# Four experts' results turned to rows by VectorE blocks and transfers in place of TensorE

## The chip, the core and the metric

The kernel runs on one core of a Trainium2 chip. The metric is the device time of one execution in microseconds (us). Engines are named as in the profile: PE is TensorE (its weight loads are PEld), DVE is VectorE, ACT is ScalarE, POOL is GpSimd, SP is SyncE, which only issues transfers here. "L889" is line 889 of the kernel. A difference of 0.2% is about 1.4 us here.

## The reference

An attention over 32 heads whose mask comes from sign hashes, followed by a mixture of experts over 3072 tokens of width 512. The change lies in the second part:

```
expert_idx = np.argmax(x @ w_gate, axis=1)           # 8 experts
for e in range(E):                                   # tokens sorted by expert
    h = np.maximum(x_sorted[lo:hi] @ w1[e], 0.0)     # 512 -> 1024
    y_sorted[lo:hi] = h @ w2[e]                      # 1024 -> 512
y = y_sorted[inv_perm]
return gate_w[:, None] * y
```

## The kernel before, in words

The first 410 us or so are the attention; while it ends, each token's row is written to the DRAM buffer `sorted_rows`, which has a region for each expert. Then the experts follow one after another in the order of how many tokens they have. Each has a fixed room (`CAPS`), and the list `PH` gives the phases: n = 0 and 1 are the largest expert in two parts of 256 tokens, n = 2 to 8 are the others with rooms for 456, 432, 408, 396, 384, 372 and 354 tokens.

The program is written out in a fixed order; each engine runs its instructions in that order and waits on semaphores. One phase n has two halves.

- **First product, `mm1(n, f)` for f = 0 to 7 (L823).** Each f is 12 matmuls of PE: 4 blocks of the depth by 3 products, since every factor is kept as a rounded value and a rest ("high" and "low") and the product of the two lows is dropped. The token block `xh` is the moving side, all tokens of the phase at once. ACT then writes the high part of `hh` (L837), DVE the low part (L839), and only then the PSUM buffer (name `s`, three of them) is free.
- **Second product, `mm2(n, m)`.** There are two forms. By token (`by_token`, rooms up to 384: phases 0, 1, 6, 7, 8) `hh` is the stationary side and the result comes out with tokens on partitions (L880). Otherwise, in the four phases n = 2 to 5 (rooms 456, 432, 408, 396), the weight is the stationary side and the result comes out as columns: 128 features on partitions, the tokens along the row (L860, 24 matmuls for each m = 0 to 3). ACT copies each to the tile `yt` (L864).

Where the result is in columns it must be turned to rows. Before, PE does it: `yout(n, j)` transposes four 128x128 blocks of `yt` into a PSUM buffer (L889), DVE scales them by the token's gate into a tile `y` (L894, three buffers), POOL sends the 128 rows to their places in the output with an indirect transfer (L896). For the four phases n = 2 to 5 these calls are spread over the next phase: after `mm1(n + 1, f)` for f = 1, 3, 5, 7.

Between these pieces stands the work for the next expert. `halves` brings its weights: SP loads half a megabyte into `raw` (L705, four buffers, three loads ahead), ACT writes the rounded part (L718), POOL the rest (L719). One such part stands behind every f of the first half of a phase, two behind every m of the second. `rows(n + 1)` loads the next tokens' rows into `xb` at the start of phase n (L735, four transfers, and `xg`, L740), and `xt_blocks(n + 1, ks)` turns them in the second half: DVE transposes 32x32 blocks (L773), ACT rounds (L774), DVE subtracts (L776). `w1p` is a second copy of w1 whose rows are in the order that these 32x32 blocks leave.

The same way of turning stands in the attention: DVE transposes 32x32 blocks (L349) and 16 transfers on SP's queue bring the blocks to other partitions (L355, `pt<-w`).

Of the kernel before, what the change touches and what calls it, by code (L numbers as in the profile page):

```python
# [7 lines left out]
F32 = mybir.dt.float32  # L8
# [13 lines left out]
DM = H * D  # L22
N = B * S
E = 8
F = 1024
# [14 lines left out]
EARLY = 256  # L40
# [11 lines left out]


@with_exitstack
def lsh_attention_moe(ctx, tc, qk, qk2, v, proj, wg, w1, w1p, w2, out):
    nc = tc.nc
    const = ctx.enter_context(tc.tile_pool(name="const", bufs=1))
    moe = ctx.enter_context(tc.tile_pool(name="moe", bufs=1))
# [494 lines left out]
    EV = {}  # L553
# [133 lines left out]
    def raw_load(c, a):  # L687

        r, k = divmod(c, 4)
        if k < 2:  # L690
            src = (w1p if r else w1)[bass.ds(EV[r], 1)].rearrange("o (a p) f -> p (o a) f", p=128)[:, 2 * a:2 * a + 2,
                                                                                k * 512:(k + 1) * 512]
        else:
            o = (k - 2) * 4 + 2 * a
            src = w2[bass.ds(EV[r], 1)].rearrange("o (a p) d -> p (o a) d", p=128)[:, o:o + 2, :]
        n = 2 * c + a
        if n in (2, 3):
            if n == 2:
                RAW["x"] = moe.tile([128, 2, 2, 512], F32, name="xhe")
            t = RAW["x"][:, a]  # L700
        elif n < 10 or n % 2:
            t = moe.tile([128, 2, 512], F32, name="raw", bufs=2)
        else:
            t = P2["p"].tile([128, 2, 512], F32, name="raw2", bufs=2)
        nc.sync.dma_start(t, src)  # L705
        RAW[c, a] = t
# [134 lines left out]
    def by_token(n):  # L841
        return PH[n][2] <= 384

    def mm2(n, m, mid=None):

        r, o, c = PH[n]
        if by_token(n):
            yout(n, m, mid)
            return
        if m == 0:  # L850
            YT[n] = (wk.tile([128, 4, EARLY], F32, name="qk") if n == 0 else
                     P2["p"].tile([128, 4, CAPS[1]], F32, name="yt"))
        h = HH[n]
        ms = slice(m * 128, (m + 1) * 128)
        p = ps.tile([128, 512], F32, name="s", bufs=3)
        k = 0
        for f in range(8):
            w = CH[4 * r + 2 + f // 4]
            for a, b in ((0, 0), (0, 1), (1, 0)):
                nc.tensor.matmul(p[:, :c], w[:, a, f % 4, ms], h[b][:, f, :c], start=(k == 0), stop=(k == 23))  # L860
                k += 1
                if k == 12 and mid:
                    mid()
        nc.scalar.activation(YT[n][:, m, :c], p[:, :c], AF.Copy)  # L864

    def yout(n, j, mid=None):
        r, o, c = PH[n]
        if j >= len(tiles_of(c)):
            return
        i, pw = tiles_of(c)[j]  # L870
        if n + 1 == len(PH) and j + 1 == len(tiles_of(c)):
            youts(n, j, i, pw)
            return
        p = ps.tile([128, 512], F32, name="s", bufs=3)
        if by_token(n):
            k = 0
            for f in range(8):
                w = CH[4 * r + 2 + f // 4]
                for a, b in ((0, 0), (1, 0), (0, 1)):
                    nc.tensor.matmul(p[:pw], HH[n][b][:, f, i:i + pw], w[:, a, f % 4],  # L880
                                     start=(k == 0), stop=(k == 23))
                    k += 1
                    if k == (12 if n else 20) and mid:
                        mid()
        else:

            yw = max(pw, min(128, CAPS[1] - i))
            for m in range(4):
                nc.tensor.transpose(p[:yw, m * 128:(m + 1) * 128], YT[n][:, m, i:i + yw], ident)  # L889
        if n:  # L890
            y = P2["p"].tile([128, DM], F32, name="y", bufs=3)
        else:
            y = moe.tile([128, DM], F32, name="y0")
        nc.vector.tensor_scalar(y[:pw], p[:pw], GT[n][:pw, j:j + 1], None, op0=OP.mult)  # L894
        nc.gpsimd.memset(C["spacer"], 0.0)
        st = nc.gpsimd.indirect_dma_start(out=out, out_offset=bass.IndirectOffsetOnAxis(ap=IX[n][:pw, j:j + 1], axis=0),  # L896
                                          in_=y[:pw], in_offset=None, bounds_check=N - 1, oob_is_err=False)
        for q in outs:
            tc.declare_no_dep(st.ins, q.ins, reason="rows of other tokens")
        outs.append(st)  # L900
# [280 lines left out]
    for n in range(1, len(PH)):  # L1181
# [3 lines left out]
            rows(n + 1)  # L1185
        for f in range(8):
            mm1(n, f)
            if f % 2 and not by_token(n - 1):
                yout(n - 1, f // 2)
            halves(c0, f)  # L1190
            if 3 <= n < 6:
                for _ in range(2):
                    next(plan, None)
        for m in range(4):
            if not last:
                xt_blocks(n + 1, ((0, 1), (2,), (3,), ())[m] if not by_token(n) else ((0, 1), (2, 3), (), ())[m])
            if not (last and m == 3):
                mm2(n, m)
            halves(c0 + 2, 2 * m)
            halves(c0 + 2, 2 * m + 1)  # L1200
        if n == 6:
# [72 lines left out]
```

## Time and profile before

| | before |
|---|---|
| median of 3 runs | 700.62 us (700.34 to 700.83) |
| the profiled execution | 699.71 us, of which the span from first to last instruction 697.8 |
| PE busy | 688.8 us (99% of the span) |
| DVE, ACT, POOL busy | 444.6, 434.3, 466.8 us (64, 62, 67%) |
| chain that ended last | PE 92%, of it 1% L889 |

A busy share of an engine says how long it had an instruction running. The chain is followed back from the last instruction to what released each step. In the four phases n = 2 to 5 and what follows them the profile page shows PE at 99% in every slice, and the clock that was granted to it at full.

### The profile page before, as it was taken

What the parts mean: (1) busy time and instruction counts of PE and PEld (TensorE: products, weight loads), DVE (VectorE), ACT (ScalarE), POOL (GpSimd) and SP (SyncE); (2) the same over time, 40 slices, a digit from 0 to 9 for tenths busy, and PEclk for the clock granted to TensorE, in tenths of its full rate; (3) what the DMA queues carried; (4) which work ended last, traced back from release to release, by engine and by line L of the source; (5) the groups of instructions that cost most, each with busy time, mean ns of one, the idle gap of its engine ahead of it and who ended that gap; (6) DMA issues with size and microseconds to landing.
All of it is one profiled execution on the core that took longest, in us unless ns stands there. A gap on an engine that the chain in (4) does not pass through costs nothing.

```text
span 697.8 us, 12285 instructions
## 1 busy us (share of the span) xinstructions
PE 688.8 (99%) x4219; PEld 564.7 (81%) x4219; DVE 444.6 (64%) x916; ACT 434.3 (62%) x866; POOL 466.8 (67%) x517
## 2 busy tenths in 40 slices
PE   8999999999999999999999999999999999999997
PEld 4778677867786778677876789899999999989896
DVE  8878787878787878788875645342939333363421
ACT  7988888878888888887876315443443444444310
POOL 7967755595796768876866436856666676758522
PEclk9999999999999999999999999999999999999999
DMA  7609777976778558764983158656355493738101
GB/s 285 160 19 261 208 219 210 269 187 219 254 230 222 154 132 224 223 202 143 257 274 129 65 184 248 170 177 155 127 163 170 131 181 123 210 124 234 61 10 42
DMA packets 64528, 123.09 MB, mean 176 GB/s; under 512 B 15329, under 2 KB 29025, under 8 KB 64400
## 3 DMA queue, kind: packets, MB, share of 16 engines
q1 hardware_dynamic: 56736, 103.17, 52.2%
q0 software_dynamic: 7584, 19.10, 8.6%
q8 instruction: 34, 0.56, 0.3%
q14 instruction: 30, 0.25, 0.1%
q10 hardware_dynamic: 144, 0.02, 0.0%
HBM read 65.75 MB, written 26.33 MB: 132 GB/s over the span
## 4 chain that ended last, share of the span: by engine, by line
PE 92%; issue 4%; POOL 1%; ACT 1%; DVE 1%; POOLq 0%
PE s L823 19%; PE t L389 18%; PE s L860 11%; PE s L297 10%; PE t L327 10%; PE s L299 9%; PE s L880 8%; PE t L409 3%; PE t L254 2%; PE s L889 1%; POOL w L719 1%; PE t L103 1%; ACT e L313 0%; POOL out_dram L896 0%; ACT pt L379 0%
## 5 line engine op out<-in xcount | busy, mean ns | idle before, releaser
L307 DVE TENSOR_SCALAR_CACHE_REDUCE e<-s 128x768 f32<-128x768 f32 x192 | 178.9, 953 | 61.3 <-PE s L299 56.5
L313 ACT ACTIVATE e<-e,m 128x768 f32<-128x768 f32 x192 | 177.9, 929 | 16.3 <-DVE e L307 12.4
L719 POOL TENSOR_TENSOR w<-raw,w 128x512 fp32r<-128x512 f32 x112 | 144.6, 1314 | 36.7 <-ACT w L718 35.5
L389 PE MATMUL t<-pt,vt 128*64 128x384 f32 x768 | 130.9, 490 | 0.0
L823 PE MATMUL s<-xh,w 128*128 128x456 f32 (+6 forms) x672 | 126.8, 346 | 0.0
L823 PEld LDWEIGHTS s<-xh,w 128*128 128x128 f32 x672 | 119.2, 188 | 3.0
L839 DVE SCALAR_TENSOR_TENSOR hh<-s,hh 128x256 fp32r<-128x256 f32 (+7 forms) x64 | 35.5, 555 | 107.5 <-ACT hh L837 107.5
L389 PEld LDWEIGHTS t<-pt,vt 128*64 128x64 f32 x768 | 52.3, 137 | 63.7 <-issue 63.2
L327 PE MATMUL t<-ident,e 128*128 128x128 f32 x648 | 92.1, 274 | 1.4 <-DVE pt L377 0.5
L379 ACT ACTIVATE pt<-t 128x512 f32<-128x512 f32 (+1 forms) x147 | 82.1, 581 | 16.4 <-PE t L327 15.3
L837 ACT ACTIVATE hh<-s 128x256 fp32r<-128x256 f32 (+7 forms) x64 | 31.3, 490 | 90.7 <-PE s L823 90.7
L327 PEld LDWEIGHTS t<-ident,e 128*128 128x128 f32 x648 | 76.6, 140 | 8.7 <-ACT e L313 1.8
L349 DVE STREAM_TRANSPOSE w<-e 128x768 f32<-128x768 f32 x84 | 79.0, 964 | 0.8 <-DMA pt<-w 0.6
L896 POOL DMA_INDIRECT out_dram<-y,ix x28 | 27.9, 996 | 73.1 <-DVE y L894 43.9
L860 PE MATMUL s<-hh,w 128*128 128x456 f32 (+3 forms) x384 | 74.9, 355 | 0.0
L860 PEld LDWEIGHTS s<-hh,w 128*128 128x128 f32 x384 | 71.1, 188 | 2.6
L718 ACT ACTIVATE w<-raw 128x512 fp32r<-128x512 f32 x112 | 66.3, 622 | 1.0 <-DMA raw<-in_w1p_dram 1.0
L880 PE MATMUL s<-w,hh 128*128 128x512 f32 (+1 forms) x240 | 56.4, 394 | 0.0
L297 PE MATMUL s<-w 80*128 80x384 f32 x192 | 55.1, 368 | 0.0
L297 PE MATMUL s<-qk 80*128 80x384 f32 x192 | 54.8, 367 | 0.0
L880 PEld LDWEIGHTS s<-w,hh 128*128 128x128 f32 (+1 forms) x240 | 44.6, 187 | 10.5
L299 PE MATMUL s<-qk 128*128 128x384 f32 x192 | 49.8, 340 | 0.0
(220 smaller groups left out, 979.9 us busy)
## 6 DMA issues: line engine op xcount, KB each, us to landing
pt<-w SPq DMA_DIRECT2D x224, 144.0 KB, 3.8
raw<-in_w_dram SPq DMA_DIRECT2D x34, 512.0 KB, 3.4
raw<-in_w1p_dram SPq DMA_DIRECT2D x28, 512.0 KB, 3.4
xd<-in_qk_dram SPq DMA_DIRECT2D x14, 768.0 KB, 7.1
sorted_rows<-xr SPq DMA_DIRECT2D x6, 1156.0 KB, 8.1
vt<-in_v_dram SPq DMA_DIRECT2D x16, 384.0 KB, 3.8
masks<-bits POOLq DMA_DIRECT2D x14, 192.0 KB, 3.8
sorted_rows<-sorted_rows SPq DMA_DIRECT2D x2, 1156.0 KB, 7.1
```

The lines of the kernel that those rows point to most:

```text
L297: nc.tensor.matmul(p[:, a, :HALF], k[0:80, 2, c], k[0:80, 3, n], start=i >= 4, stop=i < 4)
L299: nc.tensor.matmul(p[:, a, :HALF], k[:, 0, c], k[:, 1, n], start=i < 4, stop=i >= 4)
L307: nc.vector.tensor_scalar(e, SC.pop(i)[:, :, :HALF], CEIL, None, op0=OP.min, op1=OP.min, accum_out=m)
L313: nc.scalar.activation(e, e, AF.Exp, bias=m, scale=-1.0, accum_out=SM[g, hf][:, t, s:s + 1])
L327: nc.tensor.transpose(o[:, j, w], e[w][:, kt // 3, (kt % 3) * 128:(kt % 3) * 128 + 128], ident)
L349: nc.vector.transpose(z[:, :, c, w].rearrange("p g (k i) -> p g k i", i=32), e)
L379: nc.scalar.activation(o, x, AF.Copy)
L389: nc.tensor.matmul(p[s * 64:(s + 1) * 64, :HALF], VT[g][:, kt, s, :], PT[u][:, :, :, s, kt].rearrange("p a t i -> p t a i"), start=(kt == ...
L719: nc.gpsimd.tensor_tensor(w[:, 1, a], r, w[:, 0, a], op=OP.subtract)
L823: nc.tensor.matmul(p[:, :c], w[:, a, d, fs], x[:, b, d, :c], start=(k == 0), stop=(k == 11))
L860: nc.tensor.matmul(p[:, :c], w[:, a, f % 4, ms], h[b][:, f, :c], start=(k == 0), stop=(k == 23))
L880: nc.tensor.matmul(p[:pw], HH[n][b][:, f, i:i + pw], w[:, a, f % 4], start=(k == 0), stop=(k == 23))
```

## The change

The four `mm2` phases in columns keep their matmuls, but the turning to rows leaves PE. After each `mm2(n, m)` and ACT's copy to `yt`, DVE transposes `yt` in 32x32 blocks into a new tile `yb`. After m = 3, `y_rows` issues 16 transfers on SP's queue that carry the blocks between groups of 32 partitions into a new tile (same name, `yt`), in which the tokens are on partitions. DVE scales from there, no longer from PSUM. All four `yout` calls stand behind `mm1(n + 1, 7)`. A copy of w2 whose columns are ordered for this (`w2p`) is loaded for these four experts. POOL clears the few columns of `yt` beyond the tokens. In `xt_blocks` the third and fourth block are both turned at m = 1.

```diff
@@ raw_load
-            src = w2[bass.ds(EV[r], 1)].rearrange(...)[:, o:o + 2, :]
+            src = (w2 if r == 0 or by_token(r + 1) else w2p)[bass.ds(EV[r], 1)].rearrange(...)[:, o:o + 2, :]
@@ mm2
+        nb = -(-c // 32)
         if m == 0:
-            YT[n] = (wk.tile([128, 4, EARLY], F32, name="qk") if n == 0 else
-                     P2["p"].tile([128, 4, CAPS[1]], F32, name="yt"))
+            YT[n] = P2["p"].tile([128, 4, CB * 32], F32, name="yt")
+            YB[n] = P2["p"].tile([128, 4 * 4, 128], F32, name="yb")
+            nc.gpsimd.memset(YT[n][:, :, c:nb * 32], 0.0)
...
         nc.scalar.activation(YT[n][:, m, :c], p[:, :c], AF.Copy)
+        nc.vector.transpose(YB[n][:, :nb, 32 * m:32 * m + 32], YT[n][:, m, :nb * 32].rearrange("p (b j) -> p b j", j=32))
+    def y_rows(n):
+        c = PH[n][2]
+        nb = -(-c // 32)
+        YR[n] = P2["p"].tile([128, 4, DM], F32, name="yt")
+        y = YB[n].rearrange("p (t q) w -> p q t w", q=4)
+        for r in range(4):
+            for a in range(4):
+                q = (a + r) % 4
+                t = len(range(q, nb, 4))
+                nc.sync.dma_start(YR[n][32 * q:32 * q + 32, :t, 128 * a:128 * a + 128], y[32 * a:32 * a + 32, q, :t])
@@ yout
-            for m in range(4):
-                nc.tensor.transpose(p[:yw, m * 128:(m + 1) * 128], YT[n][:, m, i:i + yw], ident)
+            p = YR[n][:, j]
@@ the loop over phases
             mm1(n, f)
-            if f % 2 and not by_token(n - 1):
-                yout(n - 1, f // 2)
+            if f == 7 and not by_token(n - 1):
+                for j in range(4):
+                    yout(n - 1, j)
             halves(c0, f)
...
-                xt_blocks(n + 1, ((0, 1), (2,), (3,), ())[m] if not by_token(n) else ((0, 1), (2, 3), (), ())[m])
+                xt_blocks(n + 1, ((0, 1), (2, 3), (), ())[m])
             if not (last and m == 3):
                 mm2(n, m)
+            if m == 3 and not by_token(n):
+                y_rows(n)
             halves(c0 + 2, 2 * m)
             halves(c0 + 2, 2 * m + 1)
```

On PE the change only takes away. The first half of phase 5 (396 tokens) before, where `yt` holds the result of phase 4:

```order
L823 MATMUL s<-xh,w_6055 128x396 x24
L889 MATMUL s<-ident,yt 128x128 x4
L823 MATMUL s<-xh,w_6055 128x396 x24
L889 MATMUL s<-ident,yt 128x128 x4
L823 MATMUL s<-xh,w_6158 128x396 x24
L889 MATMUL s<-ident,yt 128x128 x4
L823 MATMUL s<-xh,w_6158 128x396 x24
L889 MATMUL s<-ident,yt 72x128 x4
```

And the same place now:

```order
L862 MATMUL s<-hh_6064,w_6000 128x408
L823 MATMUL s<-xh,w_6081 128x396 x48
L823 MATMUL s<-xh,w_6162 128x396 x48
L862 MATMUL s<-hh_6432,w_6295 128x396
L862 MATMUL s<-hh_6433,w_6295 128x396
```

The four L889 rows are gone, as in phases 3, 4 and 6, and the 96 L823 matmuls follow each other (L862 is the line that was L860).

On SP, the end of phase 2 and the start of phase 3 before, with the semaphores that each transfer waits for (DMAHW0 to 7 are the eight lanes on which SP's transfers report that they landed):

```order
L705 DMA raw<-in_w1p_dram 128x2x512 [waits DMAHW6_49,DMAHW2_49,Pool_49]
L705 ISA
L705 DMA raw_5640<-in_w1p_dram 128x2x512 [waits DMAHW7_49,DMAHW3_49,Pool_49]
L735 ISA
L735 DMA xb<-sorted_rows 32x13x128 [waits DVE_49]
```

And the same place now, the first 9 of the 16 transfers; the weight load of L705 and the four of L735 stand behind the last of them:

```order
L705 DMA raw<-in_w1p_dram 128x2x512 [waits DMAHW6_49,DMAHW2_49,Pool_49]
L881 DMA yt<-yb 32x4x128 [waits DMAHW7_49,DVE_49]
L881 DMA yt<-yb 32x4x128 x2
L881 DMA yt<-yb 32x3x128
L881 DMA yt<-yb 32x4x128 [waits DMAHW3_49]
L881 DMA yt<-yb 32x4x128 [waits DMAHW4_49]
L881 DMA yt<-yb 32x3x128 [waits DMAHW5_49]
L881 DMA yt<-yb 32x4x128 [waits DMAHW6_49]
L881 DMA yt<-yb 32x4x128 [waits DMAHW7_49]
```

The first of the 16 waits for DVE; the ninth reports on lane 7 again, as the first did, and waits until that one has landed.

On DVE, the end of the first half of phase 5 and its second half before (`y<-s` is the scaling, DMASW are the lanes of POOL's indirect transfers, whose landing frees a `y` buffer):

```order
L894 TENSOR_SCALAR y<-s,gate 128x512 [waits DMASW7_49,PE_49]
L839 SCALAR_TENSOR_TENSOR hh_6404<-s,hh_6403 128x396 [waits Activation_49] x2
L894 TENSOR_SCALAR y<-s,gate 24x512 [waits DMASW0_49,DVE_49,PE_49]
L769 COPY gate<-xg 128x3 [waits DMAHW6_49]
L751 COPY ix<-xg 128x3
L773 STREAM_TRANSPOSE xt<-xb 128x384 [waits DMAHW4_49,DMAHW5_49,DMAHW3_49,DMAHW2_49]
L773 STREAM_TRANSPOSE xt<-xb 128x384
L776 TENSOR_TENSOR xh<-xt,xh 128x384 [waits Activation_49] x2
L773 STREAM_TRANSPOSE xt<-xb 128x384
L776 TENSOR_TENSOR xh<-xt,xh 128x384 [waits Activation_49]
L773 STREAM_TRANSPOSE xt<-xb 128x384
L776 TENSOR_TENSOR xh<-xt,xh 128x384 [waits Activation_49]
```

And the same place now, from the third of the four scalings on:

```order
L908 TENSOR_SCALAR y<-yt,gate 128x512 [waits DMASW7_49]
L908 TENSOR_SCALAR y<-yt,gate 24x512 [waits DMASW0_49,DVE_49]
L769 COPY gate<-xg 128x3 [waits DMAHW6_49]
L751 COPY ix<-xg 128x3
L773 STREAM_TRANSPOSE xt<-xb 128x384 [waits DMAHW4_49,DMAHW5_49,DMAHW3_49,DMAHW2_49]
L773 STREAM_TRANSPOSE xt<-xb 128x384
L776 TENSOR_TENSOR xh<-xt,xh 128x384 [waits PE_49,Activation_49]
L776 TENSOR_TENSOR xh<-xt,xh 128x384 [waits Activation_49]
L867 STREAM_TRANSPOSE yb<-yt 128x13x32 [waits Activation_49,Pool_49]
L773 STREAM_TRANSPOSE xt<-xb 128x384 x2
L776 TENSOR_TENSOR xh<-xt,xh 128x384 [waits Activation_49] x2
L867 STREAM_TRANSPOSE yb<-yt 128x13x32 [waits Activation_49] x3
```

The four scalings now stand in a row, the fourth waiting for the transfer that the first one feeds (DMASW0), and the next tokens' transposes L773 and subtractions L776 stand behind them and, the second pair, behind a `yb` transpose too.

## Rows read from the trace of the kernel before

**Rows 1.** The page: span, busy times, PE's granted clock, and `pt` issues (KB, landing).

```profile
span 697.8 us, 12285 instructions
PE 688.8 (99%) x4219; PEld 564.7 (81%) x4219; DVE 444.6 (64%) x916; ACT 434.3 (62%) x866; POOL 466.8 (67%) x517
...
PEclk9999999999999999999999999999999999999999
...
pt<-w SPq DMA_DIRECT2D x224, 144.0 KB, 3.8
```

**Rows 2.** Groups by shape, 440 to 697.8 us: busy us, mean ns, idle before.

```profile
L889 PE MATMUL s<-ident,yt 128*128 128x128 f32 x48 | 7.2, 272 | 0.0
L889 PE MATMUL s<-ident,yt 128*72 128x128 f32 x16 | 2.4, 272 | 0.0
```

**Rows 3.** The chain that ended last, 440 us on: start, us, what.

```profile
478.95 4.71 PE s L823 x24
...
499.54 18.89 PE s L860 x96
518.43 4.49 PE s L823 x24
...
538.12 17.92 PE s L860 x96
556.04 4.32 PE s L823 x24
560.36 0.44 PE s L889 x4
...
575.10 17.34 PE s L860 x96
592.44 4.20 PE s L823 x24
...
611.01 16.67 PE s L880 x72
```

**Rows 4.** Busy by stretch (PE, PEld, DVE, ACT, POOL): phase 4's second half.

```profile
538.10:556.00 17.90, 17.90 (x98) 17.88 (x97) 9.49 (x16) 7.11 (x15) 11.70 (x10) 1.00 0.38 122
```

**Rows 5.** Groups by shape, 440 to 697.8 us, of DVE and POOL.

```profile
L896 POOL DMA_INDIRECT out_dram<-y,ix x25 | 24.9, 996 | 59.9 <-DVE y L894 30.6 <-PE s L823 5.7 <-DVE xt L773 4.6
L894 DVE TENSOR_SCALAR y<-s,gate 128x512 f32<-128x512 f32 x19 | 14.1, 744 | 17.4 <-PE s L880 17.4
L773 DVE STREAM_TRANSPOSE xt<-xb 128x448 f32<-128x448 f32 x4 | 2.4, 625 | 0.0
```

**Rows 6.** ACT in order of time, end of phase 5 and in phase 6: start, us.

```profile
592.48 0.50 ACT L864 ACTIVATE yt<-s 128x396 f32<-128x396 f32 x1 [2.79 <-PE s L860]
...
603.88 0.49 ACT L837 ACTIVATE hh<-s 128x384 fp32r<-128x384 f32 x1 [1.53 <-PE s L823]
604.26 0.62 ACT L718 ACTIVATE w<-raw 128x512 fp32r<-128x512 f32 x1
```

**Rows 7.** SP's issues in order of time, start of phase 6: start, us to the last's end.

```profile
592.37 1.89 SPq L735 DMA_DIRECT2D xb<-sorted_rows  x4
```

**Rows 8.** SP's issues in the attention: one group of 16 transfers.

```profile
50.94 11.20 SPq L355 DMA_DIRECT2D pt<-w  x16
```

**Rows 9.** Transfers, 470 to 660 us: KB each, median us to landing.

```profile
raw<-in_w1p_dram SPq DMA_DIRECT2D x19, 512.0 KB, 3.4
...
xb<-sorted_rows SPq DMA_DIRECT2D x8, 208.0 KB, 5.0
```

**Rows 10.** The indirect transfers to the output, whole span.

```profile
DMA to landing us min/median/max: 1.9/2.8/8.8
```

**Rows 11.** DVE in order of time, phases 4 and 5: start, us.

```profile
536.52 2.88 DVE L667 TENSOR_SCALAR ttt<-ttt,rof 128x24 f32<-128x24 f32 x1
...
577.73 2.16 DVE L776 TENSOR_TENSOR xh<-xt,xh 128x384 fp32r<-128x384 f32 x2 [0.19 <-ACT xh L774]
```

**Rows 12.** POOL in order of time, beside the first row above.

```profile
536.80 2.55 POOL L719 TENSOR_TENSOR w<-raw,w 128x512 fp32r<-128x512 f32 x2
```

More of the change, by code (lines that the diff above doesn't have):

```diff
@@ L54, in lsh_attention_moe @@
 @with_exitstack
-def lsh_attention_moe(ctx, tc, qk, qk2, v, proj, wg, w1, w1p, w2, out):
+def lsh_attention_moe(ctx, tc, qk, qk2, v, proj, wg, w1, w1p, w2, w2p, out):
     nc = tc.nc
@@ L694, in raw_load @@
             o = (k - 2) * 4 + 2 * a
-            src = w2[bass.ds(EV[r], 1)].rearrange("o (a p) d -> p (o a) d", p=128)[:, o:o + 2, :]
+            src = (w2 if r == 0 or by_token(r + 1) else w2p)[bass.ds(EV[r], 1)].rearrange("o (a p) d -> p (o a) d", p=128)[:, o:o + 2, :]
         n = 2 * c + a
@@ L864, in mm2 @@
         nc.scalar.activation(YT[n][:, m, :c], p[:, :c], AF.Copy)
+        nc.vector.transpose(YB[n][:, :nb, 32 * m:32 * m + 32], YT[n][:, m, :nb * 32].rearrange("p (b j) -> p b j", j=32))
+    YB, YR = {}, {}
+    def y_rows(n):
[8 more added lines that the diff above has]
+                nc.sync.dma_start(YR[n][32 * q:32 * q + 32, :t, 128 * a:128 * a + 128], y[32 * a:32 * a + 32, q, :t])
     def yout(n, j, mid=None):
@@ L873, in yout @@
             return
-        p = ps.tile([128, 512], F32, name="s", bufs=3)
         if by_token(n):
+            p = ps.tile([128, 512], F32, name="s", bufs=3)
             k = 0
@@ L885, in yout @@
         else:
-            yw = max(pw, min(128, CAPS[1] - i))
-            for m in range(4):
-                nc.tensor.transpose(p[:yw, m * 128:(m + 1) * 128], YT[n][:, m, i:i + yw], ident)
+            p = YR[n][:, j]
         if n:
@@ L1262 @@
     w1 = np.ascontiguousarray(w1).reshape(E, DM, F)
+    w2p = np.ascontiguousarray(np.asarray(inputs["moe_w2"]).reshape(E, F, 4, 4, 32).transpose(0, 1, 3, 2, 4)).reshape(E, F, DM)
     pj, wg = pj.reshape(2 * D, 32), wg.reshape(2 * D, NP, 2 * E)
@@ L1265 @@
               "in_w1_dram": np.ascontiguousarray(inputs["moe_w1"]), "in_w1p_dram": w1,
-              "in_w2_dram": np.ascontiguousarray(inputs["moe_w2"])}
+              "in_w2_dram": np.ascontiguousarray(inputs["moe_w2"]), "in_w2p_dram": w2p}
     nc = bacc.Bacc("TRN2", target_bir_lowering=False, num_devices=1, dynamic_dma_scratch_size=2048)
```

## The prediction

> **What bounds the kernel now.** I read the page's head first, for who is busy: PE has an instruction running for 688.8 of 697.8 us, the others for about two thirds, and its granted clock is full in all 40 slices [rows 1]. A busy PE alone could hide waits, so I read next, by shape, the time that PE sat idle ahead of its instructions from 440 us on: for the transposes of L889, 48 of one shape and 16 of another, it is 0.0 [rows 2]. Third, the chain that ended last, in order of time: in phases 3 to 6 it never leaves PE. Twenty-four L823 matmuls, 0.44 us of L889, twenty-four L823 matmuls, and so on, each piece starting where the one ahead ends [rows 3]. So in these phases every microsecond that PE doesn't need comes off the end, unless a new wait takes its place.
>
> **What is removed.** The chain has 16 pieces of L889 of 0.44 us, four in each of phases 3 to 6, one of which is shown [rows 3]: 16 x 0.44 = 7.0 us, 64 transposes at 0.11 each. The mean of 272 ns that the groups show [rows 2] is no price: 64 x 272 ns = 17.4 us would be the most that one could claim, but these durations overlap with the neighbours (pipelined instructions), and the starts in the chain leave only 0.44 from one piece to the next. I take 7.0. The matmuls on both sides keep shape and number. Also gone are four uses of a PSUM buffer in each of these phases; since PE didn't wait for one, that is worth nothing.
>
> **What is added, engine by engine.** I count within a phase from E, PE's end of the last second product of the phase ahead, and from E', PE's end of the first product. Without L889, E' - E is four times the L823 piece of the phase: 4 x 4.71 = 18.8, 4 x 4.49 = 18.0, 4 x 4.32 = 17.3 and 4 x 4.20 = 16.8 us in phases 3, 4, 5, 6; the second product behind E' takes 18.9, 17.9, 17.3 and 16.7 [rows 3].
>
> DVE gets 16 transposes of 32x32 blocks. The nearest row is the same operation on 448 columns, 625 ns [rows 5]; at that price four per expert are 2.5 us. They fall in the second half of a phase, where DVE is busy 9.5 of 17.9 us [rows 4]: hidden. POOL's clearing of at most 24 columns a block is four small instructions, between nothing and 1.3 us (one of the two L719 that took 2.55 [rows 12]), in a half where POOL has 11.7 of 17.9 us to do [rows 4]: hidden too. Loading w2p for w2 is as many bytes in as many transfers. The scalings read another memory now; 744 ns [rows 5] is the price from PSUM, and I keep it.
>
> **SP's queue** is where the change could bite. The 16 transfers wait for the last `yb` transpose: E, plus 0.50 for ACT's copy [rows 6], 0.6 for DVE's transpose [rows 5], some 0.2 of hand-over, so E + 1.3. Behind them on SP stand one weight load, the four `xb` loads and `xg`, then the next weight load. How long do 16 issues take? Nearest in size of a piece (512 bytes) and in partitions (32) are the `xb` loads: four in 1.89 us, 0.47 each [rows 7], which makes 7.6. Nearest in purpose are the attention's 16 `pt` transfers: 11.2 us [rows 8], but those carry 144 KB each [rows 1] and these 64 KB at most. The order shows that the ninth waits until the first has landed, which after eight issues (3.8 us) and a landing of up to 5.0 [rows 9] adds at most 1.2. I take 8.0 (bounds 7.6 and 11.2). So the weight load goes out at E + 9.3 and lands 3.4 later [rows 9], at E + 12.7. ACT wants it behind its fifth `hh` write, as the fifth first product ends at 5/8 of E' - E and the write takes 0.49 [rows 6]: E + 12.3, 11.7, 11.3 and 11.0 in the four phases. ACT will thus stand for 0.4 to 1.7 us.
>
> That is hidden by PSUM. PE goes on through the sixth, seventh and eighth first product in three buffers and needs ACT's sixth write, with DVE's low part behind it, only at E'. Behind the landing come one conversion of 0.62, the write of 0.49 [rows 6] and DVE's part, as long again, some 0.6: 1.7 in all, so E + 14.4 against E' at E + 16.8 at the earliest. Cover left: 2.4 us in phase 6, 4.4 in phase 3. The next weight load, behind the `xb` loads and `xg` (1.89 for the four [rows 7], a fifth as long as one of them), lands some 3 us later, at E + 15.7; what hangs on it (the eighth write) PE wants only at the 22nd matmul of the second product, 3.6 us behind E'. Covered as well, and the `xb` rows are not needed before E'.
>
> **DVE's burst.** All four scalings now stand behind the eighth low part, and the next tokens' transposes behind them. From E': ACT's write and DVE's low part 1.1; three scalings 2.2, so 3.3. The fourth needs a `y` buffer, that is, the landing of the first's transfer: that goes out at 1.9, with 1.0 on POOL [rows 5] and 2.8 to landing [rows 10], so at most 5.7; the fourth ends at 6.5. Then two transposes (1.2), two subtractions (2.2 for such a pair [rows 11]), one `yb` transpose (0.6), two transposes and two subtractions again: E' + 13.9, and ACT's rounding of the third block between them makes it some 14.5. PE wants `xh` complete at the next phase's start, E' + 16.7 at the earliest. Cover left: 2.2 us at the least. ACT's first copy to `yt`, which waits for the fourth scaling too and stands behind ACT's rounding of the first two blocks, comes at about E' + 8.7; PE comes back to that PSUM buffer at three quarters of the second product, E' + 12.5 at the earliest. Nothing is paid.
>
> The **sum**: the profiled execution took 699.71 us, its span 697.8, and 1.9 lie around it; 699.71 - 7.0 = 692.7. It lay 0.9 below the median of the runs, 700.62, so the forecast for the median is 693.6 us.
>
> **A rule against the change.** The row says that 128x128 transposes on PE cost 0.11 us of the path each while DVE has eight free microseconds in every half phase [rows 3, 4]. The Trainium skill (VectorE: DVE Perf Modes, Rules for kernel authors) advises TensorE for a 128x128 transpose where PSUM will do as destination. By that rule taken alone nothing would be gained, 700.6 us; it looks at the operation, the chain at who is late, and here the chain decides.
>
> **The rivals.**
>
> *SP's transfers hold the weights back (the other side).* For it: the attention's 16 took 11.2 us [rows 8]. At that price the load lands at E + 15.9, ACT's sixth write and its low part are done at E + 17.6, and PE stands 0, 0, 0.3 and 0.8 us: 1.1 in all, 694.7. Each further microsecond costs PE up to four. The gain is used up when the four stalls sum to 7.0, that is, at a mean of 1.75; since E' - E is 17.7 on average, the load must land at E + 17.75, which means 16 transfers in 13.1 us, 0.82 each. From there on the kernel is slower than before: at 1.0 each (16 us, landing at E + 20.7) the stalls are 3.6, 4.4, 5.1, 5.6 and the time 693.6 + 18.7 = 712.3. Against it: no row has more than 0.70 a transfer, and those carried more than twice as much.
>
> *DVE's burst comes too late for the next tokens.* For it: a landing of an output transfer has taken 8.8 us [rows 10], and a DVE instruction on 24 columns of SBUF has taken 2.88 us while two of POOL's L719 ran [rows 11, 12]; the scalings read SBUF now. Six microseconds more on the first landing put `xh` at E' + 20.5. PE reads the fourth block's low part first with its eleventh matmul, 1.9 us into the phase, so the four phases would stand 0, 0.7, 1.3 and 1.9: 3.9 us, 697.5, if it came every time; if in one phase, 695. Against it: at that point POOL has no L719 to run but waits for the scalings itself.
> The Trainium skill (SBUF — State Buffer, Who interferes with whom) gives the reason for such rows: VectorE and GpSimd share a pair of ports that one holds for a whole instruction, `tensor_scalar` with SBUF on both sides among those that may take it. The trace agrees for the 2.88 us; that the scalings will be hit is open.
>
> *PE's time is not the limit after all.* If POOL or the transfers set the pace, nothing is gained: 700.6. Against it: POOL has 6 us free in a half phase [rows 4], and the idle time ahead of PE's rows is 0.0.
>
> **How the numbers follow.** PE's 7.0 us come off, stalls below 0.6 in all: 0.74, with 693.0 to 694.2 as that case's own range. Mild stalls from SP or from the burst, 694.2 to 699: 0.16. The gain is eaten up, no change: 0.04. Slower, by SP's transfers or both stalls together: 0.06. To leave out no more than 2 in 10 the range goes down to 692.9 (the spread of the runs) and up to 697.0, near the burst's price in all four phases and past that of the 11.2 us. 0.2% is 1.4 us, about what a measurement here tells from no change; faster by more than that is below 699.2: 0.74 + 0.16 = 0.90, same 0.04, slower 0.06. The time predicted is that of the likeliest case, 693.6.
>
> **What the changed profile would show.** If I am right: no L889 row, PE's idle time ahead of L823 and the second product still 0.0, the chain on PE from 440 to 660 us, phases 3 to 6 shorter by 1.75 us each; on SP 16 issues in 7.6 to 9 us, each group beginning some 1.3 us behind the second product; on ACT a wait of a microsecond for a weight load ahead of the fifth conversion of a first half; on DVE the fourth scaling three microseconds behind the third. I would be wrong if PE's first matmul of a second product waited for ACT or DVE (the SP rival), if the first product of phases 4 to 7 waited for `xh` (the burst), or if all phases were shorter and the end no earlier.

## The result, and the profile after

The change makes the kernel **slower**: 710.5 us median (710.23 to 711.27 in four runs) against 700.65 in the same sitting, a ratio of 1.0143 with a 95% interval of 1.0125 to 1.016. Forecast were 693.6, with a range to 697.0. The profiled execution took 710.54 us, its span is 708.7.

From the page of the kernel after: span, busy times, PE's busy tenths and granted clock in 40 slices, and the new transfers and the spill table (KB each, median us to landing). They answer to [rows 1].

```profile
span 708.7 us, 12270 instructions
PE 687.0 (97%) x4155; PEld 559.4 (79%) x4155; DVE 446.7 (63%) x932; ACT 433.1 (61%) x866; POOL 466.8 (66%) x521
...
PE   8999999999999999999999999999999968999997
...
PEclk9999999999999999999999999999999998999999
...
yt<-yb SPq DMA_DIRECT2D x28, 64.0 KB, 2.1
yt<-yb SPq DMA_DIRECT2D x36, 48.0 KB, 2.0
...
spill_rows<-tab SPq DMA_DIRECT2D x1, 24.0 KB, 11.3
```

PE has 64 instructions fewer, and its row has a hole that was not there (before, every slice from 440 us on but the last shows a 9, which stands for 90% or more): two slices of 6 and 8 tenths from 567 us on, and the granted clock's only 8 in the second of them. What it waited for, by line (PE's waits from 440 us on: us in total, times, the longest):

```profile
PE s L862 <- ACT hh L837: 9.3, 3, 7.6
PE s L862 <- DVE hh L839: 1.6, 3, 1.2
PE s L897 <- DVE hh L839: 1.4, 1, 1.4
PE s L823 <- DVE xh L776: 0.3, 1, 0.3
```

12.6 us in all, where [rows 2] and the chain of [rows 3] had none. 12.3 of them stand ahead of the second product (L862, and L897 in phase 6), for `hh`. So the transposes went as forecast, and new waits took more than they gave. The chain that ended last now leaves PE in phases 3 to 6; here it is through phase 3 (start us, us, what), to set beside [rows 3]:

```profile
480.81 0.69 DVE yb L867
481.51 0.68 SPq L881
...
485.46 1.76 SPq L881
...
492.41 0.60 SPq L881
...
496.60 6.33 DMA raw<-in_w1p_dram
502.95 0.63 ACT w L718
503.58 0.43 ACT hh L837
504.03 0.62 DVE hh L839
504.69 14.83 PE s L862 x74
```

Read it backwards: 74 matmuls of the second product waited for DVE's low part, that for ACT's high part, that for ACT's conversion of a weight, and that for a weight load which took 6.33 us to land and was issued late because 16 row transfers stood ahead of it. SP's issues in order of time, phases 3 and 5 (start us, us to the last's end):

```profile
481.51 11.50 SPq L881 DMA_DIRECT2D yt<-yb  x16
493.27 0.38 SPq L705 DMA_DIRECT2D raw<-in_w1p_dram  x1
493.86 1.91 SPq L735 DMA_DIRECT2D xb<-sorted_rows  x4
495.95 0.39 SPq L740 DMA_DIRECT2D xg<-sorted_rows  x1
496.60 0.39 SPq L705 DMA_DIRECT2D raw<-in_w1p_dram  x1
...
558.04 11.25 SPq L881 DMA_DIRECT2D yt<-yb  x16
569.55 0.38 SPq L705 DMA_DIRECT2D raw<-in_w1p_dram  x1
570.13 1.90 SPq L735 DMA_DIRECT2D xb<-sorted_rows  x4
572.22 0.51 SPq L740 DMA_DIRECT2D xg<-sorted_rows  x1
572.83 0.43 SPq L677 DMA_DIRECT2D spill_rows<-tab  x1
573.52 3.49 SPq L705 DMA_DIRECT2D raw<-in_w1p_dram  x1
```

Sixteen take 11.5, 10.55, 11.25 and 10.7 us in the four phases. I call the weight load right behind them the first, and the one behind `xb` and `xg` the second. In phase 5 one more transfer stands ahead of the second: the table of spill rows, 24 KB, which took 11.3 us to land. That load was issued at 573.52, SP stood at its issue for 3.49 us, and ACT got it at 585.87, 12.3 us after the issue began. PE's answer, phases 3 and 5, in order of time (the idle time ahead of each piece and its releaser in brackets):

```profile
504.05 0.46 PE L862 MATMUL s<-hh,w 128*128 128x432 f32 x1 [0.92 <-ACT hh L837]
...
575.33 4.06 PE L862 MATMUL s<-hh,w 128*128 128x396 f32 x21 [1.22 <-DVE hh L839]
586.94 15.35 PE L862 MATMUL s<-hh,w 128*128 128x396 f32 x75 [7.55 <-ACT hh L837]
```

In phase 5 PE stops twice: ahead of the second product for the first load, and at the 22nd matmul, as the prediction counted, for the second. The second stop is the long one. Phases 3 and 4 have the second stop alone, phase 6 the first alone (1.41 us). Behind the long stop the clock is lower; by stretch (busy us of PE, PEld, DVE, ACT, POOL, then the granted clock, DMA share, GB/s):

```profile
582.00:590.00 8.00, 3.06 (x8) 2.75 (x9) 2.03 (x4) 1.54 (x3) 2.65 (x5) 0.58 0.79 230
...
586.94:602.13 15.19, 15.19 (x75) 14.88 (x76) 11.80 (x18) 5.91 (x13) 10.08 (x14) 0.90 0.49 171
```

A mean of 0.58 of 2.4 GHz says that PE was at 1.2 GHz for most of the eight microseconds around the restart; 0.90 that it still was for a part of the 15 from the restart on.

**Where the 10.9 us of span went.** The length of a phase is the time from its first L823 matmul to that of the next, from PE's timeline of each kernel (in us; for "no transfers" and the other columns see the experiments):

| phase | before | after | no transfers (e1) | first load ahead (e7) | in fours (e8) | table in rows (e10) | fours + rows (e11) |
|---|---|---|---|---|---|---|---|
| 3 | 39.48 | 39.33 | 37.71 | 37.72 | 37.71 | 38.84 | 37.72 |
| 4 | 37.61 | 37.31 | 35.90 | 39.40 | 35.90 | 37.29 | 35.89 |
| 5 | 36.40 | 45.47 | 34.61 | 44.09 | 40.08 | 39.42 | 34.61 |
| 6 | 35.23 | 35.37 | 33.47 | 36.09 | 33.48 | 34.89 | 33.48 |
| 7 | 32.94 | 33.80 | 32.94 | 33.57 | 34.37 | 33.79 | 34.07 |

Phases 3 to 6 sum to 148.72 before and 157.48 after: +8.8. Phase 7 adds 0.9, and phase 3 starts 1.2 later (480.02 against 478.79 us), which is 10.9. That last 1.2 is no work of the change, as far as the runs tell: phase 3 starts between 478.5 and 480.2 us in the kernels below, without a pattern.

### The profile page after: what moved, and what is told of

It is laid out like the page before. It is cut to its first block, busy times and chain, and to the rows that moved or that the text cites. A ratio compares the mean times of both kernels' runs of the same rounds, so it can differ in the third digit from the quotient of the medians.

```text
span 708.7 us, 12270 instructions
## 1 busy us (share of the span) xinstructions
PE 687.0 (97%) x4155; PEld 559.4 (79%) x4155; DVE 446.7 (63%) x932; ACT 433.1 (61%) x866; POOL 466.8 (66%) x521
## 2 busy tenths in 40 slices
DMA packets 72593, 126.71 MB, mean 179 GB/s; under 512 B 16353, under 2 KB 37089, under 8 KB 72464
## 4 chain that ended last, share of the span: by engine, by line
PE 68%; SPq 8%; issue 8%; DMA 6%; POOL 6%; ACT 3%; DVE 1%; POOLq 0%; ACTq 0%
PE t L389 17%; PE s L297 9%; PE t L327 9%; PE s L299 9%; PE s L862 7%; PE s L823 6%; SPq L881 6%; PE s L897 5%; DMA raw<-in_w1p_dram 5%; POOL w L719 4%; PE t L409 3%; SPq L355 2%; PE t L254 1%; DMA xd<-in_qk_dram 1%; POOL out_dram L910 1%
## 5 line engine op out<-in xcount | busy, mean ns | idle before, releaser
L719 POOL TENSOR_TENSOR w<-raw,w 128x512 fp32r<-128x512 f32 x112 | 143.2, 1305 | 71.4 <-ACT w L718 70.7
L313 ACT ACTIVATE e<-e,m 128x768 f32<-128x768 f32 x192 | 177.9, 930 | 16.3 <-DVE e L307 12.3
L823 PE MATMUL s<-xh,w 128*128 128x456 f32 (+6 forms) x672 | 124.3, 345 | 0.3 <-DVE xh L776 0.3
L823 PEld LDWEIGHTS s<-xh,w 128*128 128x128 f32 x672 | 119.9, 188 | 4.1 <-DVE xh L776 0.6
L862 PE MATMUL s<-hh,w 128*128 128x456 f32 (+3 forms) x384 | 77.5, 361 | 10.8 <-ACT hh L837 9.3
L862 PEld LDWEIGHTS s<-hh,w 128*128 128x128 f32 x384 | 72.2, 191 | 15.7 <-ACT hh L837 10.3
L897 PE MATMUL s<-w,hh 128*128 128x512 f32 (+1 forms) x240 | 56.6, 395 | 1.4 <-DVE hh L839 1.4
L897 PEld LDWEIGHTS s<-w,hh 128*128 128x128 f32 (+1 forms) x240 | 44.5, 187 | 12.6 <-DVE hh L839 2.0
## 6 DMA issues: line engine op xcount, KB each, us to landing
xd<-in_qk_dram SPq DMA_DIRECT2D x14, 768.0 KB, 10.2
```

The source lines that it names most:

```text
L313: nc.scalar.activation(e, e, AF.Exp, bias=m, scale=-1.0, accum_out=SM[g, hf][:, t, s:s + 1])
L719: nc.gpsimd.tensor_tensor(w[:, 1, a], r, w[:, 0, a], op=OP.subtract)
L823: nc.tensor.matmul(p[:, :c], w[:, a, d, fs], x[:, b, d, :c], start=(k == 0), stop=(k == 11))
```

## The experiments

All times are medians with the ratio to the kernel before in the same sitting, whose median was 700.35 to 700.69 us. The expectations weigh three theories: A, the place of the 16 transfers on SP's queue; B, DVE's burst; C, the added traffic, wherever it is issued.

### The transfers taken away, and put where nothing else is changed

**e1_no_transfers.** The kernel after, but the scalings read the 32x32 blocks as DVE left them, and the 64 transfers are gone. The output's rows are in another order; everything else runs.

```diff
-        YR[n] = P2["p"].tile([128, 4, DM], F32, name="yt")
-        y = YB[n].rearrange("p (t q) w -> p q t w", q=4)
...
-                nc.sync.dma_start(YR[n][32 * q:32 * q + 32, :t, 128 * a:128 * a + 128], y[32 * a:32 * a + 32, q, :t])
+        YR[n] = [YB[n][:, min(4 * j, nb - 4):min(4 * j, nb - 4) + 4].rearrange("p q w -> p (q w)") for j in range(4)]
```

> The changed kernel without its 64 transfers between partitions: the scalings read the 32x32 blocks where VectorE left them, so the output rows are mixed up; all else stands. Theory A (the 16 transfers of a phase hold SyncE's queue and the weight loads behind them come late): TensorE's waits for ScalarE and VectorE at the second products go away, the 7.0 us of the removed transposes show in full, 693 to 695 us. Theory B (the four scalings in a row make VectorE late for the next tokens): the burst is still there, 705 us or more. Theory C (the extra traffic slows the weight loads wherever it is issued): as A.

Measured: 693.28 us, ratio 0.9906 (0.9889 to 0.9922). PE waits for nothing from 440 us on, and phases 3 to 6 are 1.77, 1.71, 1.79 and 1.76 us shorter than before: 7.03, the 7.0 of the prediction. DVE's burst is all there; its timeline in phase 4 (second product from 534.39 to 552.31):

```profile
535.63 1.27 DVE L902 TENSOR_SCALAR y<-yb,gate 128x512 f32<-128x512 f32 x3
539.26 0.48 DVE L902 TENSOR_SCALAR y<-yb,gate 48x512 f32<-48x512 f32 x1 [2.36 <-DMA out_dram<-y,ix]
...
545.08 1.70 DVE L776 TENSOR_TENSOR xh<-xt,xh 128x396 fp32r<-128x396 f32 x2
```

`xh` is complete at 546.78, 12.4 us behind the start of the second product (forecast 14.5) and 5.5 ahead of the next phase. So the transfers are the whole loss, and the burst none of it.

**e5_before_plus_16.** The kernel before, with 16 transfers of 64 KB on SP at the end of phases 2 to 5, into a tile that nobody reads.

```diff
+            if m == 3 and not by_token(n):
+                yd = P2["p"].tile([128, 4, 4, 128], F32, name="yd")
...
+                        nc.sync.dma_start(yd[32 * q:32 * q + 32, :, a], YT[n][32 * a:32 * a + 32, :, 128 * q:128 * q + 128] ...
```

> The kernel before, with TensorE's transposes as they were, plus 16 transfers of 64 KB between partitions at the end of each of phases 2 to 5, into a tile that nobody reads. Theory A: TensorE's first product is 1.75 us longer than in the changed kernel and covers the waits of 1 to 1.5 us in phases 3, 4 and 6; in phase 5 some 7 us of wait and 1.8 us of clock remain, 707 to 711 us. Theory B: no burst, 700.6 us. Theory C: 702 us or more, spread over all four phases.

Measured: 717.18 us, ratio 1.0244 (1.0227 to 1.0261): past the 707 to 711 of theory A and not the 700.6 of theory B; theory C set no upper end, but had the loss spread over all four phases. In the trace, of a run of 714.3 us, PE, which waited for nothing before, waits 9.6 us from 440 us on, 5.8 of them in phase 5:

```profile
588.57 11.68 PE L860 MATMUL s<-hh,w 128*128 128x396 f32 x49 [5.83 <-ACT hh L837]
```

The transfers alone, with PE's transposes still there, cost more than the whole change: +16.5 us against +9.9. That is about what they cost in the change itself, 17.2 (693.28 in e1 to 710.5), so the 1.75 us that PE's transposes add to each phase, which theory A had expected to cover the waits outside phase 5, covered little: 3.0 us by the traces (12.6 to 9.6).

### Their number or their bytes

**e9_sixteen_small.** The kernel of e1 with 16 transfers of 16 KB put back, a quarter of the bytes; as there, the output's rows are mixed.

```diff
+        yd = P2["p"].tile([128, 4, 128], F32, name="yd")
...
+                nc.sync.dma_start(yd[32 * q:32 * q + 32, a], YB[n][32 * a:32 * a + 32, q])
```

> The kernel without the 64 transfers (scalings read the 32x32 blocks, 693.3 us, rows in another order) with 16 transfers of 16 KB each put back where they stood, a quarter of the bytes, into a tile that nobody reads. If the number of transfers on SP is what counts: 16 still take 9 to 11 us there and the time is 703 to 711. If their bytes count: 16 take below 6 us, and the time is 693 to 697.

Measured: 708.39 us, ratio 1.0118 (1.0093 to 1.0143). SP's timeline in phase 3, and PE's in phase 5:

```profile
481.37 11.00 SPq L880 DMA_DIRECT2D yd<-yb  x16
...
586.45 16.49 PE L862 MATMUL s<-hh,w 128*128 128x396 f32 x75 [9.43 <-ACT hh L837]
```

A quarter of the bytes, and the same 10 to 11 us and much the same waits (10.5 us in all). It is the number that counts: SP gets through 16 in 10.2 to 11.5 us, whether of 16, 48 or 64 KB.

### Which load ends last

**e7_first_load_ahead.** The row transfers one weight load later.

```diff
-            if m == 3 and not by_token(n):
-                y_rows(n)
             halves(c0 + 2, 2 * m)
             halves(c0 + 2, 2 * m + 1)
+            if m == 3 and not by_token(n):
+                y_rows(n)
```

> The changed kernel with only the first of the two weight loads moved ahead of the 16 transfers; the second stays behind them and the token rows. If, as the chain of the changed kernel reads, the second load is what ends last (issue at E + 16.4, landing 6.3 us later), this helps little: PE's waits stay at 9 to 13 us and the time is 707 to 711. If the first load was what held PE, as the prediction's rival had it, the waits go to below 3 us and the time to 695 to 699.

Measured: 709.95 us, ratio 1.0156 (1.0123 to 1.0188): no gain, as the chain said. The phases tell more than the sum: phase 3 has lost its waits (37.72 us, as in e1), phase 4 is 2.1 us longer than in the kernel after, since behind its stop of 1.33 us PE's granted clock is 0.89 for 15.4 us, and phase 5 still waits for the second load:

```profile
540.42 0.46 PE L862 MATMUL s<-hh,w 128*128 128x408 f32 x1 [1.33 <-ACT hh L837]
...
584.77 15.54 PE L862 MATMUL s<-hh,w 128*128 128x396 f32 x73 [7.12 <-ACT hh L837]
```

**e2_after_f1.** All 16 behind the second load too, after the second group of the next first product.

```diff
+            if f == 1 and not by_token(n - 1):
+                y_rows(n - 1)
...
-            if m == 3 and not by_token(n):
-                y_rows(n)
```

> The changed kernel with the same 64 transfers, but each group of 16 issued in the next phase behind the weight load that follows the second first product (f = 1), so that three loads and the next tokens' rows go out ahead of it. Theory A (place on SyncE's queue): the weight loads land before ScalarE wants them, 693.5 to 697 us. Theory B (burst): as the changed kernel, 705 to 711. Theory C (traffic): the same bytes move in the same phase, 705 to 711.

Measured: 704.56 us, ratio 1.0065 (1.0043 to 1.0088). Phases 3 and 4 have no waits any more. In phases 5 and 6 the rows themselves are now late: DVE stands for them, and PE then for `yt` and `xh`. DVE in phase 5:

```profile
576.89 1.28 DVE L908 TENSOR_SCALAR y<-yt,gate 128x512 f32<-128x512 f32 x3 [5.52 <-DMA yt<-yb]
583.81 0.47 DVE L908 TENSOR_SCALAR y<-yt,gate 24x512 f32<-24x512 f32 x1 [5.64 <-DMA out_dram<-y,ix]
```

So the transfers can make the loads behind them late, or come too late for their own readers; between the two there is little room.

**e6_loads_one_earlier.** Every weight load one step earlier, so that the first stands ahead of the 16 and the second where the first was.

```diff
-                h = 2 * n + k // 2 + 3
+                h = 2 * n + k // 2 + 4
+                if h == 12:
+                    h = 11
...
+    raw_load(6, 0)
```

> The changed kernel with every weight load from the first product of phase 1 on issued one step (two weight blocks) earlier, as soon as its own buffer is converted; buffers, transfers and the 16 row transfers stay. The load that stood right behind the 16 now stands ahead of them, and the one that stood behind the token rows now stands where that one was. Theory A (PE waits because weight loads stand behind the 16 transfers on SP, and the later of the two ends last): the 12.6 us of PE waits fall to 2 to 6, most of them left in phase 5 where the spill table's transfer still holds a load back; 696 to 702 us. Theory B (the 16 transfers slow everything that moves, whatever stands behind them): the waits stay above 9 us and the time is 706 to 711.

Measured: 703.36 us, ratio 1.0058 (1.0037 to 1.0079), a little above what I expected. Phases 3 and 4 are again as in e1. Phase 5 is 3.7 us longer than there: the fourth scaling waits 8.56 us for the first one's rows to land in the output, and ACT's `yt` copy, which PE waits for, stands behind it. This is the burst's rival, about as long as the longest landing of [rows 10]. The same wait is 5.39, 6.02 and 6.08 us in phases 3, 4 and 6; the spill table, issued at 570.81, is on its way in phase 5 alone, and no run here separates its part from that of the loads. Phase 6 is 1.9 us longer; phase 7 has a wait of 2.7 us for `xh` near its start and is 5.6 us longer.

### The spill table

**e4_table_late.** The table's transfer some 32 planning steps later, so at the end of phase 6.

```diff
+        for _ in range(32):
+            yield
         nc.sync.dma_start(tabd.rearrange("t p c -> p t c"), tab)
```

> The changed kernel with one small transfer (the spill table, 24 KB in short pieces, which landed in 11.3 us ahead of a weight load in phase 5) moved to the end of phase 6. Theory A, with this transfer as what makes phase 5 the worst: the wait of 8.8 us in phase 5 falls to the 1 us of phases 3 and 4 and the 1.8 us of lower clock behind it go, 700 to 702 us. Theory B: 709 to 711. Theory C without a part for the table: 709 to 711.

Measured: 710.06 us, ratio 1.0148 (1.012 to 1.0176). Phase 5's long wait is gone, but PE now stops in phases 6 and 7 (in order of time):

```profile
611.08 18.50 PE L899 MATMUL s<-w,hh 128*128 128x512 f32 x72 [2.33 <-DVE hh L841]
656.05 13.70 PE L899 MATMUL s<-w,hh 128*128 128x512 f32 x51 [5.36 <-ACT hh L839]
```

The second stop moved along with the table: SP issues it at 638.58, takes 3.75 and 3.44 us for the `xb` and `xg` behind it (1.9 and 0.39 elsewhere), and ACT gets the load behind those 7.8 us after its issue. The first stop is not the table's, which is not yet issued; it is the first load's, 1.41 us in the kernel after. So the sum alone, which lies where theories B and C had it, decides nothing; the next run does.

**e10_table_rows.** The table at its old place, but laid out by partition, so that a partition writes 192 bytes in a row and not 24 pieces of 8.

```diff
-    tabd = nc.dram_tensor("spill_rows", [TMAX, 128, 2], I32).ap()
+    tabd = nc.dram_tensor("spill_rows", [128, TMAX, 2], I32).ap()
...
-        nc.sync.dma_start(tabd.rearrange("t p c -> p t c"), tab)
+        nc.sync.dma_start(tabd, tab)
```

> The changed kernel with the spill table written partition by partition (192 bytes in a row) instead of in pieces of 8 bytes; everything else as it is. If the table's transfer is what holds the weight load behind it in phase 5 (landing 11.3 us before), its landing falls below 4 us, the 7.55 us wait of phase 5 and the clock's drop after it go, and PE's waits fall from 12.6 to 4 to 6 us: 700 to 704 us. If the 16 transfers alone make phase 5's wait, nothing changes: 708 to 711.

Measured: 701.92 us, ratio 1.0021 (1.0012 to 1.0031). 2,944 packets under 512 bytes are gone (16,353 to 13,409), SP issues the second load of phase 5 in 0.38 us, not 3.49, and ACT gets it at 578.07, 5.7 us after its issue at 572.36, not 12.3. PE's waits are 5.4 us in all, and the longest is now

```profile
579.14 0.45 PE L862 MATMUL s<-hh,w 128*128 128x396 f32 x1 [1.70 <-ACT hh L837]
```

So by the medians 8.6 of the change's 17.2 us above e1 go with the table's pieces, and 8.6 remain with the 16 transfers. By the traces 6.05 us of the first part lie in phase 5 (45.47 to 39.42); of what remains, 4.8 lie there too (39.42 against 34.61 in e1). The time lost to the lower clock is not the table's: behind the wait of 1.70 us the granted clock is 0.89 over 15.15 us, much as in the kernel after.

**e13_before_table_rows.** The same edit in the kernel before.

> The kernel before with nothing but the spill table written partition by partition. Before, PE waited for nothing in phase 5, so the table's slow transfer was covered there: if the gain of the version in fours comes from PE's transposes and not from the table, this stays at 700.6 within 1 us. If the table alone was worth something, it is faster by more than 1.4 us, and the change's share in the best version is smaller by that.

Measured: 699.89 us, ratio 0.9991 (0.9983 to 1.0): nothing that could be told from no change. Before, the table took 9.1 us to land and the load behind it, issued at 560.46, took 10.2; both were covered.

### Both mended

**e8_in_fours.** The first load and the token rows first, then eight of the 16, four more behind the next group of PE's first product, the second load, and the last four.

```diff
+            if f < 3 and not by_token(n - 1):
+                for r in ((0, 1), (2,), (3,))[f]:
+                    y_rows(n - 1, r)
             halves(c0, f)
...
-            if m == 3 and not by_token(n):
-                y_rows(n)
```

> The changed kernel with the 16 transfers cut up: the first weight load and the token rows go ahead, eight of the 16 after the first PE product of the next phase, then the second weight load, then four and four. Theory A: each load waits behind at most eight transfers, so PE's waits fall to 2 to 6 us, phase 5's spill table again the largest; 695 to 701 us. Rival (late rows): the rows land so late that the scalings and the next tokens' blocks come late, as where all 16 went after the second load (704.6 us): 702 to 706. Theory B: 706 to 711.

Measured: 700.21 us, ratio 0.9995 (0.998 to 1.0009). Phases 3, 4 and 6 are as in e1; only phase 5, with the table, is 5.5 us longer (a wait of 3.25, and a granted clock of 0.89 over the 15 us behind it), and phase 7 1.4. (In the trace twelve transfers stand ahead of the second load, not eight as the expectation says.)

**e11_in_fours_table_rows.** e8 with the table of e10.

> The 16 transfers cut up between the weight loads (700.2 us) and the spill table written partition by partition. Theory A: phase 5's 3.3 us wait and what the clock loses behind it go, PE's waits fall below 1.5 us and the time is 694 to 697, faster than both kernels by what the prediction took for the change. Rival: the late rows of phases 5 and 6 take the wait's place: 698 to 701.

Measured: **694.62 us**, ratio 0.9919 (0.9906 to 0.9932): faster than both kernels. One wait is left, at the start of phase 7 (first row, PE's waits from 440 us on); behind it SP's issues of phase 5:

```profile
PE s L823 <- DVE xh L776: 0.5, 1, 0.5
```

```profile
558.00 6.08 SPq L881 DMA_DIRECT2D yt<-yb  x8
564.19 0.53 SPq L677 DMA_DIRECT2D spill_rows<-tab  x1
564.77 2.52 SPq L881 DMA_DIRECT2D yt<-yb  x4
567.54 0.39 SPq L705 DMA_DIRECT2D raw<-in_w1p_dram  x1
567.97 2.52 SPq L881 DMA_DIRECT2D yt<-yb  x4
```

The second load goes out at 567.54, six microseconds earlier than in the kernel after. Phases 3 to 6 are as in e1 to a hundredth; phase 7 is 1.1 longer. All 64 transfers with all their bytes are there, and so is the burst, so neither of theories B and C is the loss: it is the order on SP's queue, and the table in it.

**e12_fours_table_early.** e11 with the earlier loads of e6.

> As the kernel in fours with the table written partition by partition, and every weight load one step earlier too. If what is left there is still weight loads, this takes the rest away: 693 to 695. If it is late rows, this does not help, or costs a little, since one more load stands ahead of the row transfers: 695 to 699.

Measured: 701.54 us, ratio 1.0025 (1.0006 to 1.0043), with the twelve runs from 699.17 to 707.01: worse than either expectation. The trace is of a run of 700.82. With one more weight load ahead of them the token rows go out at 484.53 us in phase 3 (479.71 in e11), and the 16 behind them. In phase 6 DVE waits 7.07 us for the rows; the next tokens come late, PE stands 2.72 us in the first product of phase 7, and the 17.94 us behind that run at a granted clock of 0.84.

## Why the prediction was wrong, step by step

**What bounds the kernel** was right: PE, with no wait. **What is removed** was right: 7.03 us in e1 against 7.0, and e1 at 693.28 is the forecast of 693.6 without the transfers. **DVE's burst**, POOL's clearing and `w2p` cost nothing in e1; the scalings were even cheaper than taken. The reason given against the burst's rival, that POOL has no L719 to run then, holds for the scalings of e1 but not for the subtractions behind them: in phase 5 two of these took 5.02 us beside three L719, not 2.2, and `xh` was still complete 3.1 us ahead of the next phase.

**SP's queue** is the step that failed, in three terms.

*The 16 issues.* I took 8.0 us by the price of the `xb` loads, 0.47 each. They take 10.55 to 11.5, the price of the attention's `pt` [rows 8], which I called "nearest in purpose" and set aside because those carry more bytes. e9 shows that bytes do not enter. Both move data from SBUF to SBUF; that this likeness sets the price is not shown (the last section has other transfers at 0.6 us). With 11.5 the first load is issued 13.1 us behind E in phase 3 (forecast 9.3), and ACT has it at E + 16.7 (E + 12.7).

*The second load.* "Lands some 3 us later, at E + 15.7 ... covered as well." In phase 3, where E is 480.2, it was issued at E + 16.4, later than I had it landing, and ACT got it at E + 22.7. Of the 7.0 us 4.1 are its issue, and 2.9 its landing in 6.33 instead of the 3.4 of [rows 9]. Most of these 2.9 are not the work of the 16: in e1, without them, the same load took 5.3, 5.1 and 5.6 us to land in phases 3, 4 and 6. The 3.4 is a median over all loads, and this one, behind `xb` and `xg`, was never that fast there. PE wanted what hangs on it 3.6 us behind E', so about E + 22.4. The rival *SP's transfers hold the weights back* came true, but I priced it with the first load alone: 694.7 at 11.2 us, and a break-even at 0.82 us per transfer. At 0.66 to 0.72 per transfer the kernel was already 1.4% slower. The first load's own stops, 1.22 and 1.41 us in phases 5 and 6, are no more than 2.6 of the 12.6, and e7 shows that it is not what decides: ahead of the 16, it changes the sum by nothing.

*The table.* The prediction lists what stands behind the transfers and leaves out the table of spill rows, which is issued in phase 5 between `xg` and the second load. Before, it was issued at 559.8 us and harmed nobody (e13), though the load behind it took 10.2 us to land there, and 11.9 in e1. Behind the 16, where that load takes 12.3, it has no slack left: the slowness was there before, and the change uncovered it. In pieces of 8 bytes the table costs 8.6 us (after against e10), of which the traces show 6.05 in phase 5, where the longest wait is 7.55 against 1.70; the rest lies in phases without the table, and no run explains it. Phase 5 of the kernel after is 10.86 us longer than in e1: 8.77 of waits, and some 2.1 in which the matmuls ran longer, most of that at the lower clock, which e10 has as well.
The Trainium skill (DMA: Bandwidth & Descriptors, Why small descriptors are slow (HBM only)) states a fixed overhead for each packet that weighs on small pieces to or from HBM, and not on SBUF to SBUF. The runs agree with the direction of the first half, as the load behind the table came 12.3 us after its issue with pieces of 8 bytes and 5.7 with pieces of 192; whether that overhead is the reason is not shown, and no run here tries small pieces from SBUF to SBUF.

**PE's time is not the limit after all** did not come true: e1 has all of the 7.0.

**The rule against the change** (the Trainium skill, VectorE: DVE Perf Modes, Rules for kernel authors: TensorE for a 128x128 transpose) gave 700.6 and the better side of the forecast, but not for a reason that the runs bear out: e11 gains 5.7 us (700.35 to 694.62) by leaving TensorE, once SP's order and the table are mended; some 5 of them are left against e13, which has the same table (ratios 0.9919 and 0.9991).

The 1.1 us of phase 7 in e11, of which 0.54 is PE's wait, look like any stop at full clock here: a phase with one is some 0.5 us longer than the wait that the profile shows (phase 3 of the kernel after 1.62 longer than in e1 with 1.10 of waits, phase 7 of e8 1.43 with 0.89).

What is left open: why a load behind `xb` and `xg` takes 5 us to land even without the 16, and the one more that it takes with them; why SP needs 0.6 us for some transfers and less for others; and whether fewer transfers, or another engine's queue, would do, since every kernel here that moves the blocks has 16 for each expert on SP's.

## What to carry to other kernels

When work goes onto a queue that issues in order, list every transfer behind it up to the second and third that someone waits for, and price each with the landing that it has at its own place in the trace, not with a median over all; here the load right behind the new work was not the one that ended last. Price the issue of transfers by the row that is like them in all but size, and count them before their bytes. And a transfer that nobody waits for is not free: it has a place in the queue, and the change decides whom it stands ahead of.

## What the runs showed of the hardware that I had not expected

- SP takes 0.6 us to issue one of these transfers from SBUF to SBUF, whatever its size, and 0.37 to 0.39 for a weight load of 512 KB from DRAM that waits for nothing. By tile (duration on SP in ns, least, median and most), of the kernel after and of e9:

```profile
L881 SPq DMA_DIRECT2D yt<-yb x64: 592/599/1764, 481.5 to 614.2; - x64
```

```profile
L880 SPq DMA_DIRECT2D yd<-yb x64: 512/589/1576, 481.4 to 613.8; - x64
```

  The attention's `pt` of 144 KB has 512/591/1579 in the trace of before: the price that I needed stood there. The two memories alone do not give the price: in the same trace the median is 0.33 us for `xb` and 0.57 for the attention's `xd` of 768 KB, both from DRAM to SBUF, and about 0.6 for `sorted_rows`, from SBUF to DRAM (0.606) and within DRAM (0.590).
- The clock did not fall by every wait: after 0.92 and 0.18 us in phase 3 of the kernel after, and after 1.41 us in its phase 6, the following 15 us have a granted clock of 1.00; after 1.33 us in phase 4 of e7 it is 0.89, and after 1.70 us in phase 5 of e10 too, after 7.55 us 0.90; after 2.72 us in e12, behind a piece of seven matmuls, 0.84 over 17.9 us. So the length of the wait alone does not decide, and a short one can cost as much clock as a long one.
- A scaling of 128x512 from SBUF is cheaper than from PSUM; groups by shape of the kernel after, from 440 us on (busy us, mean ns, idle before):

```profile
L908 DVE TENSOR_SCALAR y<-yt,gate 128x512 f32<-128x512 f32 x12 | 5.9, 542 | 0.1
L908 DVE TENSOR_SCALAR y<-s,gate 128x512 f32<-128x512 f32 x8 | 5.9, 742 | 9.4 <-PE s L897 9.4
```

- Two subtractions for `xh` that took 2.16 us before [rows 11] took 5.00 while POOL ran three of its subtractions (593.22 to 597.1 us), without PE waiting (DVE in order of time, phase 5 of the kernel after):

```profile
593.04 5.00 DVE L776 TENSOR_TENSOR xh<-xt,xh 128x384 fp32r<-128x384 f32 x2 [0.19 <-ACT xh L774]
```

The Trainium skill (SBUF — State Buffer, Who interferes with whom) has a DVE instruction with two inputs in SBUF contend with GpSimd's reads there; this row agrees. The other traces add which of the two starts first: where DVE's first subtraction starts 0.2 us ahead of POOL's, the pair takes 5.00 to 5.02 us (the kernel after, e1, e10); where POOL's starts 0.05 to 0.07 us ahead, 3.22 to 3.26 (e2, e6, e8, e11, e12) beside as many of POOL's; before, beside one of them, 2.16.
